# Two 512-token chunks of an MLP mixer joined into one of 1024 tokens, on one core

## Chip, cores and metric

The kernel runs on one core of a Trainium2 chip. The metric is the device time of one execution in microseconds (us); runs of a kernel are summed up by their median. An execution can also be profiled: the profile's span runs from the first to the last instruction of the program, and the execution's own time lies a little above it.

## What is computed

Memory attention for 8 batches of 576 tokens, then a token-mixing and a channel-mixing layer. The change lies in the channel mixing (the last line) and in the order of the work at the start of the program.

```python
# _attn_ref, per batch and head: 32 memory slots from phi, k, v; softmax attention of q over the slots
x = attn_out.transpose(0, 2, 1, 3).reshape(8, 576, 512)
xt = x.transpose(0, 2, 1)
h = np.maximum(xt @ w_tok1, 0.0) @ w_tok2          # token mixing, 576 -> 256 -> 576
u = x + h.transpose(0, 2, 1)
h2 = np.maximum(u @ w_ch1, 0.0) @ w_ch2            # channel mixing, 512 -> 1536 -> 512
return u + h2
```

## The kernel before

**Chunks.** The 8 x 576 = 4608 tokens are cut into 9 chunks of 512 (`CW`), numbered 0 to 8; `HW` is 256. For each chunk the channel mixing runs layer 1 (512 to 1536 channels, in 12 hidden blocks of 128, taken as 6 pairs `p`) and layer 2 (back to 512). Each product is written in float32 as three matmuls on halves: high x high, high x low, low x high. ScalarE (ACT) makes a high half by a copy, VectorE (DVE) the low half by a subtraction. TensorE (PE) is the engine that all of this feeds; its sums stand in PSUM banks of 512 float32 columns.

**Three forms.** Chunks 0 to 2 (`Chunk`) multiply plainly, with matmuls of 512 columns (lines 159 and 182). Chunks 3 to 6 (`Quarters`) do layer 1 by seven quarter products instead of eight: a block matrix of two by two, with sums and differences of the blocks (Winograd's form: products named 11, T1, 21, T2, 22, T3, T4), which take 256 columns, half of the chunk's tokens, each (line 320); layer 2 stays plain. Chunks 7 and 8 (`Sevens`, driven by `seven`) do both layers by seven products of 256 columns: layer 1 at line 420 into one PSUM tile `one`, layer 2 at line 373 into the tiles `m` and `mT`. For each pair, layer 1 of the pair is interleaved on PE with layer 2 of the pair before it (`mix`). Layer 2 of the last pair of chunk 8 is plain (line 402). A quarter product is 6 matmuls: two halves of 128 of its inner or its output side, times the three combinations.

**Sums of weights.** Seven products need sums of the weights too. Those of `w_ch1` are made once (`Sums`), stored in DRAM and loaded per pair as units (`load_unit`, 3 ahead). Those of `w_ch2` (`Tops`, four blocks a pair, each in high and low) are made by DVE and ACT from half-step 156 on and stay in rooms of SBUF that other tiles have left.

**Order.** From the first product on, a half-step counter `h` orders the work by hand: `at(h, fn)` puts a step at a half-step, `MOVES` shifts single steps, and each step is recorded on its engine's queue in that order. There are 24 half-steps a chunk, 4 a pair; chunk 7 begins at half-step 168. The split of the chunk's input into blocks and halves (`t1` to `t4`, `high`, `low`) stands in the 15 half-steps ahead of the chunk. Before the first product, in the front, a planner inside the program (`plan`) orders some 390 steps (the attention of batches 0 and 1, the weights' unpacking): it holds a cost for each step and picks, at each turn, the free step of the highest rank. Ranks came from seeded draws (`SEEDS`). Where it sees PE idle, it puts filler matmuls of the identity (line 1242).

Of the kernel before, what the change touches and what calls it, by code (L numbers as in the profile page):

```python
# [10 lines left out]
F32 = mybir.dt.float32  # L11
# [9 lines left out]
P = 128  # L21
# [7 lines left out]
def kernel(  # L29
# [188 lines left out]
    class Quarters(Chunk):  # L218
# [3 lines left out]
        def __init__(s, c):  # L222
            s.c, s.n, s.hid, s.x = c, f"_{c}", {}, {}
            s.u = s.o = wide(F32, "u" + s.n)
            s.end = NF - (2 if c == CHUNKS - 1 else 0)
# [99 lines left out]
    class Sevens(Quarters):  # L325

        banks = {}  # L330
        rooms2 = {}

        def left(s, name, p):
            if name in s.tops[p]:
                return s.tops[p][name]
            i, j = {"11": (0, 0), "21": (0, 1), "T4": (1, 1)}[name]
            return [x[p][:, j, HW * i : HW * i + HW] for x in (c2h, c2l)]

        def open_banks(s):
            tags = [(pat, "at", 2)] * 2 + [(pacc, f"acc{a}", 1) for a in range(NKK)] + [(pch, "ch", 2)]  # L340
            for name, (pool, tag, n) in zip(("11", "22", "T1", "T3", "T2", "21", "T4"), tags):
                s.banks[name] = pool.tile([P, 2, HW], F32, tag=tag, name="m" + name, bufs=n)

        def open_rooms(s):
            r = s.rooms2
            for name, tag in (("st2", "hh"), ("st3", "hl"), ("11", "hh"), ("22", "hl"), ("21", "al"), ("V", "al")):
                r[name] = sb.tile([P, 2, HW], F32R, tag=tag, name="r" + name, bufs=2)
            for name, tags in (("T13", ("ah", "ah")), ("T24", ("Rh", "Rl"))):
                r[name] = [
                    sb.tile([P, 2, HW], F32R, tag=tag, name=f"r{name}{x}", bufs=2 if tag == "ah" else 1)  # L350
                    for x, tag in enumerate(tags)
                ]
            for name, x in (("T1", 0), ("T3", 1), ("T2", 2), ("T4", 3)):
                r[name] = [t[:, x % 2] for t in r[("T13", "T24")[x // 2]]]
            Sevens.T = {
                name: sb.tile([P, HW], F32, tag=tag, name="s" + name, bufs=1)
                for name, tag in (("T1", "Ah"), ("T3", "Al"), ("T2", "vb"))
            }

        def right(s, name):  # L360
            r = s.rooms2[name]
            return (r[:, 0], r[:, 1]) if name[0] != "T" else r

        def seconds(s, p):

            for name in ("11", "22", "T1", "T3", "T2", "21", "T4"):
                lh, ll = s.left(name, p)
                h, l = s.right(name)
                for a in range(2):
                    for x, (l_, r) in enumerate(((lh, h), (lh, l), (ll, h))):  # L370
                        first, last = not (a or x or p), a == 1 and x == 2
                        yield name if last else None, lambda name=name, a=a, l_=l_, r=r, first=first: (
                            nc.tensor.matmul(  # L373
                                s.banks[name][:, a], l_[:, a * P : a * P + P], r,
                                start=first, stop=False, skip_group_check=True,
                            )
                        )

        def drain(s, name):
            V, m = f32(s.rooms2["V"]), s.banks  # L380

            def add(to, x):
                o = s.quarter(int(to[0]) - 1, int(to[1]) - 1) if to != "V" else V
                return lambda: nc.vector.tensor_tensor(out=o, in0=x, in1=o, op=ALU.add)

            return {
                "11": [lambda: nc.scalar.copy(out=V, in_=m["11"]), add("11", m["11"])],
                "22": [add("12", m["22"])],
                "T1": [add("12", m["T1"]), add("22", m["T1"])],
                "T3": [],  # L390
                "T2": [add("V", m["T2"]), add("12", V), add("V", m["T3"]), add("22", V), add("21", V)],
                "21": [add("11", m["21"])],
                "T4": [add("21", m["T4"])],
            }[name]

        def direct(s, i, t, fs, ps, start=False):

            for a in range(2):
                for n, f in enumerate(fs):
                    h, l = s.hid[f]  # L400
                    for x, (l_, r) in enumerate(((c2h, h), (c2h, l), (c2l, h))):
                        nc.tensor.matmul(
                            ps[:, a],
                            l_[f // 2][:, f % 2, (2 * i + a) * P : (2 * i + a + 1) * P],
                            r[:, t * HW : (t + 1) * HW],
                            start=start and not (a or n or x), stop=False, skip_group_check=True,
                        )

        def first(s, ps, weights, name, start):
            mm = [  # L410
                (l[:, a], r[:, a])
                for a in range(2)
                for l, r in (
                    (weights[:, 0], s.x[name][0]),
                    (weights[:, 0], s.x[name][1]),
                    (weights[:, 1], s.x[name][0]),
                )
            ]
            for n, (l, r) in enumerate(mm):
                nc.tensor.matmul(ps, l, r, start=start and n == 0, stop=False, skip_group_check=True)  # L420

    class Tops:
# [5 lines left out]
        def words(s):  # L428
            s.w = sb.tile([P, 2, DM], F32, tag="big", name=f"cw{s.p}", bufs=1)
            for j in range(2):  # L430
                yield lambda j=j: nc.vector.tensor_tensor(
                    out=s.w[:, j], in0=f32(c2h[s.p][:, j]), in1=f32(c2l[s.p][:, j]), op=ALU.add
                )

        def rooms(s):
            def quad(pool, tag):
                return pool.tile([P, 4, HW], F32R, tag=tag, name=f"top{tag}", bufs=1)

            if s.p in (0, 5):
                tag = ("kv", "rest")[s.p // 5]  # L440
                t = sb.tile([P, 2, 4, HW], F32R, tag=tag, name=f"top{tag}", bufs=1)
                s.pieces = [(t[:, 0, o], t[:, 1, o]) for o in range(4)]
                s.merged = [(t[:, 0, o : o + 2], t[:, 1, o : o + 2]) for o in (0, 2)]
            elif s.p < 3:
                h, l = (quad(wp, f"w{s.p}{x}") for x in "hl")
                s.pieces = [(h[:, o], l[:, o]) for o in range(4)]
                s.merged = [(h[:, o : o + 2], l[:, o : o + 2]) for o in (0, 2)]
            elif s.p == 4:
                h = quad(sb, "qT")
                l = [  # L450
                    sb.tile([P, HW], F32R, tag=tag, name=f"top{tag}{x}", bufs=2)
                    for tag in ("vh", "vl") for x in range(2)
                ]
                s.merged = None
                s.pieces = [(h[:, o], l[o]) for o in range(4)]
            else:
                s.merged, s.pieces = None, []
                for x, (tag, n) in enumerate((("phi", 2), ("phi", 2), ("S", 1), ("aT", 1))):
                    t = sb.tile([P, 2, HW], F32R, tag=tag, name=f"top{tag}{x}", bufs=n)
                    s.pieces.append((t[:, 0], t[:, 1]))  # L460
            Sevens.tops[s.p] = dict(zip(("T2", "T3", "22", "T1"), s.pieces))

        def steps(s):

            yield from s.words()
            s.rooms()
            a11, a21, a12, a22 = w = [s.w[:, j, HW * i : HW * i + HW] for j in range(2) for i in range(2)]
# [7 lines left out]
            parts = [(h, l, x) for (h, l), x in zip(s.pieces, w)]  # L475
            if s.merged:
                parts = [
                    (h, l, s.w[:, j].rearrange("p (i n) -> p i n", i=2)) for j, (h, l) in enumerate(s.merged)
                ]
            for h, l, x in parts:  # L480
                yield lambda h=h, x=x: nc.scalar.copy(out=h, in_=x)
            for h, l, x in parts:
                yield lambda h=h, l=l, x=x: nc.vector.tensor_tensor(out=l, in0=x, in1=f32(h), op=ALU.subtract)

    Sevens.tops = {}
    chunks = {}

    def mixer(c):
        if c not in chunks:
            chunks[c] = (Chunk if c < WIN else Quarters if c < CHUNKS - 2 else Sevens)(c)  # L490
        return chunks[c]
# [1976 lines left out]
```

## Time and profile before

| what | value |
| --- | --- |
| median of 3 runs | 745.89 us (745.12 to 746.94) |
| the profiled execution: its own time, its span | 746.36 us, 744.5 us |
| PE, DVE, ACT, POOL busy | 736.8, 518.3, 371.0, 84.0 us |
| PE instructions | 5387 |
| granted TensorE clock | 0.9 of full speed or more in each of 40 slices |
| DMA | 147.40 MB, mean 198 GB/s |

PE, DVE, ACT and POOL are TensorE, VectorE, ScalarE and GpSimd; PEld is TensorE's loading of weights, which overlaps its matmuls; SP issues DMAs. A matmul's duration in a row is longer than its turn on the engine, since matmuls are pipelined: its price is read from the distance between the starts of equal ones. The same holds, with a smaller overlap, for DVE and ACT.

### The profile page before, as it was taken

What the parts mean: (1) busy time and instruction counts of PE and PEld (TensorE: products, weight loads), DVE (VectorE), ACT (ScalarE), POOL (GpSimd) and SP (SyncE); (2) the same over time, 40 slices, a digit from 0 to 9 for tenths busy, and PEclk for the clock granted to TensorE, in tenths of its full rate; (3) what the DMA queues carried; (4) which work ended last, traced back from release to release, by engine and by line L of the source; (5) the groups of instructions that cost most, each with busy time, mean ns of one, the idle gap of its engine ahead of it and who ended that gap; (6) DMA issues with size and microseconds to landing.
All of it is one profiled execution on the core that took longest, in us unless ns stands there. A gap on an engine that the chain in (4) does not pass through costs nothing.

```text
span 744.5 us, 14081 instructions
## 1 busy us (share of the span) xinstructions
PE 736.8 (99%) x5387; PEld 655.3 (88%) x5387; DVE 518.3 (70%) x1032; ACT 371.0 (50%) x845; POOL 84.0 (11%) x79
## 2 busy tenths in 40 slices
PE   8999999999999999999999999999999999999997
PEld 8787788787878888998998989888989999999997
DVE  4989864788567757774776568664856478889646
ACT  5889774242414334553644436353635354656452
POOL 1114434002112122000000000000001000000000
PEclk9999999999999999999999999999999999999999
DMA  8965540575826355786777858683756467656741
GB/s 351 396 234 190 198 126 11 145 249 168 280 54 229 108 182 180 243 229 216 183 251 226 270 150 274 202 268 120 217 204 188 117 182 252 207 160 206 245 150 57
DMA packets 90835, 147.40 MB, mean 198 GB/s; under 512 B 41488, under 2 KB 61072, under 8 KB 86544
## 3 DMA queue, kind: packets, MB, share of 16 engines
q1 hardware_dynamic: 74496, 99.81, 41.1%
q10 hardware_dynamic: 16272, 46.68, 20.0%
q8 instruction: 43, 0.70, 0.4%
q14 instruction: 24, 0.20, 0.1%
HBM read 121.57 MB, written 24.90 MB: 197 GB/s over the span
## 4 chain that ended last, share of the span: by engine, by line
PE 95%; DMA 2%; DVE 2%; SPq 0%; issue 0%; ACT 0%; DVEq 0%
PE acc L182 31%; PE cp L159 13%; PE qa L320 9%; PE one L420 8%; PE u L908 8%; PE qb L320 7%; PE mT L373 4%; PE Ap L868 3%; PE m L373 3%; PE Rp L887 1%; PE sp L725 1%; DMA kv<-in_kv_dram 1%; PE sp L626 1%; PE u L1566 1%; PE kvp L626 1%; DMA rows<-S 1%
## 5 line engine op out<-in xcount | busy, mean ns | idle before, releaser
L182 PE MATMUL acc<-qhh,c 128*128 128x512 f32 x256 | 99.2, 396 | 0.0
L182 PE MATMUL acc<-hh,c 128*128 128x512 f32 x288 | 96.6, 394 | 0.0
L320 PEld LDWEIGHTS qa<-xT,unit 128*128 128x128 f32 x432 | 61.1, 188 | 6.5 <-ACT whole L2140 0.3
L320 PEld LDWEIGHTS qb<-x,unit 128*128 128x128 f32 x432 | 61.1, 188 | 6.3
L182 PEld LDWEIGHTS acc<-hh,c 128*128 128x128 f32 x288 | 54.1, 188 | 14.1 <-issue 2.9
L320 PE MATMUL qa<-xT,unit 128*128 128x256 f32 x432 | 62.9, 281 | 0.0
L320 PE MATMUL qb<-x,unit 128*128 128x256 f32 x432 | 62.8, 281 | 0.0
L182 PEld LDWEIGHTS acc<-qhh,c 128*128 128x128 f32 x256 | 48.2, 188 | 9.3 <-issue 3.3
L182 PE MATMUL acc<-hl,c 128*128 128x512 f32 x144 | 56.2, 390 | 0.0
L182 PE MATMUL acc<-qal,c 128*128 128x512 f32 x192 | 54.5, 394 | 0.0
L2143 DVE TENSOR_TENSOR whole<-whole 128x256 f32<-128x256 f32 x48 | 20.6, 430 | 44.5 <-ACT whole L2140 44.5
L159 PE MATMUL cp<-uh,c1h 128*128 128x512 f32 x144 | 51.5, 398 | 0.0
L182 PE MATMUL acc<-qhl,c 128*128 128x512 f32 x128 | 50.7, 396 | 0.0
L2140 ACT COPY whole<-qa 128x256 f32<-128x256 f32 x72 | 26.7, 371 | 48.1 <-PE qa L320 46.1
L159 PE MATMUL cp<-ul,c1h 128*128 128x512 f32 x144 | 50.3, 390 | 0.0
L159 PE MATMUL cp<-uh,c1l 128*128 128x512 f32 x144 | 50.3, 390 | 0.0
L127 DVE SCALAR_TENSOR_TENSOR hl<-cp,hh 128x512 fp32r<-128x512 f32 x36 | 24.8, 688 | 30.3 <-ACT hh L124 30.2
L420 PE MATMUL one<-x,unit 128*128 128x256 f32 x288 | 40.5, 283 | 0.0
L420 PEld LDWEIGHTS one<-x,unit 128*128 128x128 f32 x288 | 37.3, 192 | 0.4 <-ACT whole L2292 0.2
L2140 ACT COPY whole<-qb 128x256 f32<-128x256 f32 x48 | 17.8, 370 | 38.4 <-PE qb L320 38.4
L182 PEld LDWEIGHTS acc<-qal,c 128*128 128x128 f32 x192 | 32.2, 189 | 2.9
L925 ACT COPY rest<-u 128x288 f32<-128x288 f32 (+8 forms) x48 | 15.3, 318 | 37.6 <-PE u L908 36.8
(343 smaller groups left out, 1812.4 us busy)
## 6 DMA issues: line engine op xcount, KB each, us to landing
unit<-sums ACTq DMA_DIRECT2D x75, 512.0 KB, 4.1
unit<-sums SPq DMA_DIRECT2D x33, 512.0 KB, 4.4
kv<-in_kv_dram SPq DMA_DIRECT2D x12, 1280.0 KB, 8.2
rawc<-in_w_ch_dram SPq DMA_DIRECT2D x12, 1024.0 KB, 7.1
q<-in_q_dram SPq DMA_DIRECT2D x16, 576.0 KB, 6.5
unit<-sums ACTq DMA_DIRECT2D x25, 256.0 KB, 3.7
sums<-sums SPq DMA_DIRECT2D x12, 512.0 KB, 5.7
phi<-in_phi_dram SPq DMA_DIRECT2D x16, 320.0 KB, 4.8
```

The costliest lines, as they stand in the source:

```text
L127: nc.vector.scalar_tensor_tensor(out=l, in0=ps, scalar=0.0, in1=f32(h), op0=ALU.max, op1=ALU.subtract)
L159: nc.tensor.matmul(ps, l[:, a, w], r[:, a], start=n == 0, stop=n == len(mm) - 1)
L182: nc.tensor.matmul(ps, l_[f // 2][:, f % 2, a * P : (a + 1) * P], r[:, w], start=f == start and x == 0, stop=f == end - 1 and x == 2,)
L320: nc.tensor.matmul(ps[:, :HW], l, r, start=first and n == 0, stop=n == len(mm) - 1, skip_group_check=not first,)
L373: nc.tensor.matmul(s.banks[name][:, a], l_[:, a * P : a * P + P], r, start=first, stop=False, skip_group_check=True,)
L420: nc.tensor.matmul(ps, l, r, start=start and n == 0, stop=False, skip_group_check=True)
L626: nc.tensor.matmul(s.kvp[32 * i : 32 * i + 32, : 2 * D], s.pt[:, i, j, :], s.kv[:, :, j, i, :], start=j == 0, stop=j == NC - 1,)
L868: nc.tensor.matmul(ps[:, :TT], a, w, start=x == 0, stop=x == len(mm) - 1)
L908: nc.tensor.matmul(ps[:, :HALF], a, r, start=x == 0, stop=x == len(mm) - 1)
L925: nc.scalar.copy(out=rest[0][:, kk, o : o + HALF - n], in_=ps[:, n:HALF])
L2140: nc.scalar.copy(out=to, in_=ps[:, :HW])
L2143: nc.vector.tensor_tensor(out=to, in0=x, in1=y, op=ALU.add)
```

## The change

Chunks 7 and 8 are taken as one pair of chunks (`Pair`, 1024 tokens): the two column blocks of the seven products are the two chunks, so a quarter product has 512 columns. First layer 1 of all six pairs `p` runs (line 393 of the changed file), and its results `hid` stay in SBUF, 24 tiles of 512 columns; then layer 2 runs (`second`, line 2233), 42 steps `k` of two groups of three matmuls. Right sides of layer 2 are split into high and low by `prepare`, 6 steps ahead (`LEAD`). Chunk 8's input and output live in the tile `rest`. `Tops` now stores its blocks in DRAM; pair 0's are made in the half-steps ahead of layer 1, the others during layer 1, and `load_tops` brings all of them back once layer 2 has begun. In the last product (T4) the second output half runs as two pieces of 256 columns.

The planner takes a fixed rank and engine for each step (`RANKS`) in place of drawn ones, with other costs for DMA and overlap; the count of fillers follows a new formula, and some entries of `MOVES` change.

```diff
-    class Sevens(Quarters):
...
+    class Pair(Quarters):
...
+        def quarter(s, k, t):
+            return (s.u, rest[0])[t][:, 2 * k : 2 * k + 2]
...
+        def product(s, ps, weights, name, first, end):
             mm = [
-                (l[:, a], r[:, a])
+                (l[:, a], r[a])
                 for a in range(2)
...
+                    ps, l, r, start=first and n == 0, stop=n == len(mm) - 1,
...
+                    for x, t in enumerate((h, w)):
+                        nc.sync.dma_start(out=tops[s.p][:, x, o], in_=f32(t))
...
-    def plan(seeds):
...
+    OVERLAP = {"ACT": 0.09, "DVE": 0.07}
+
+    def plan(ranks):
...
-                landed = max(landed, z.begin + 2.2) + 1.08 * z.move
+                landed = max(landed, z.begin + 2.2) + 0.91 * z.move + 1.6 * (z is first_loads[2])
...
+    RANKS = (
+        778, 776, 772, 756, 780, 770, 774, 754, 748, 704, 702, 554, 728, 446, 366, 102,
...
+    PAIR = [
+        (-15, "t1"), (-15, "high", "11"), (-14.5, "high", "T1"), (-13, "low", "11"), (-10.5, "low", "T1"),
+        (-6.5, "t3"), (-6, "high", "21"), (-5.5, "t2"), (-5, "high", "T3"), (-4, "high", "T2"), (-4, "low", "T3"),
+        (-3.5, "low", "21"), (-3, "t4"), (-2.5, "high", "22"), (-2.5, "low", "T2"), (-2, "high", "T4"),
+        (-1.5, "low", "22"), (-1, "low", "T4"),
+    ]
...
-        shares = (12, 12, 12, 12) if begin else (11, 11, 11, 9)
...
+    STEPS = (("11", "U"), ("T1", "B"), ("21", "A"), ("T2", "U"), ("22", "B"), ("T3", "U"), ("T4", "D"))
+    TOPS, banks, LEAD = {}, {}, 6
+
+    def second(k, a, w=slice(0, CW)):
+        (name, room), p = STEPS[k // (NF // 2)], k % (NF // 2)
+        (lh, ll), r = left_rows(name, p), ring[k]
+        h, l = r[:, 0, w], r[:, 1, w]
+        for x, (l_, r_) in enumerate(((lh, h), (lh, l), (ll, h))):
...
+    def last_part(p):
+        a = start_a.pop()
+        first(p, 6, a, "T4", False)
+        relu(hid["21", p], a)
...
+        first(p, 1, b1, "21", True)
+        if p:
+            add(hid["22", p - 1], start_a[0], hid["22", p - 1])
...
+        if p:
+            last_part(p - 1)
...
+        a = pch.tile([P, CW], F32, tag="ch", name=f"m11{p}", bufs=2)
+        first(p, 0, a, "11", True)
+        nc.scalar.copy(out=hid["11", p], in_=a)
+        add(hid["11", p], b1, hid["11", p])
...
+        b2 = pat.tile([P, CW], F32, tag="at", name=f"mT1{p}", bufs=2)
+        first(p, 3, b2, "T1", True)
...
+        first(p, 2, a, "T2", False)
+        nc.scalar.copy(out=hid["12", p], in_=a)
...
+        first(p, 5, b2, "22", False)
...
+        first(p, 4, a, "T3", False)
...
+    for k in range(6 * n):
+        for a in range(2):
+            second(k, a)
+        if k == 1:
+            last_part(p)
+            load_tops()
...
+        prepare(k + LEAD)
+        for fn in side.pop(k, ()):
+            fn()
```

Where it moves instructions shows at three places. First PE, in the last stage: pair 1 of chunk 8 before, layer 1 of the joined chunks (`m`, `mT`) and the begin of layer 2 (`mU`) in the change; `c` and `top...` are weights, `r`, `rT`, `x` and `xT` right sides.

```order
L373 MATMUL m_6982<-r_6875,topw2h 128x256 x2
L373 MATMUL m_6982<-r_6875,topw2l 128x256
L373 MATMUL mT_6983<-rT_6878,topw2h 128x256
L373 MATMUL mT_6983<-rT_6879,topw2h 128x256
L373 MATMUL mT_6983<-rT_6878,topw2l 128x256
L420 MATMUL one<-x_7_6856,unit_7226 128x256 x6
L420 MATMUL one<-xT_7_6809,unit_7200 128x256 x6
L373 MATMUL mT_6983<-rT_6879,topw2h 128x256
```

```order
L393 MATMUL m_7089<-x_6398,unit_7010 128x512 x6
L393 MATMUL mT_7101<-xT_6410,unit_7034 128x512 x6
L393 MATMUL m_7089<-xw1h,unit_7034 128x512
L393 MATMUL m_7089<-xw1l,unit_7034 128x512
L2233 MATMUL mU_7384<-r_7343,c_578 128x512 x3
L2233 MATMUL mU_7385<-r_7343,c_578 128x512 x3
L2233 MATMUL mU_7384<-r_7353,c_701 128x512 x3
```

Each matmul has 512 columns instead of 256, and the two layers no longer take turns.

Second DVE, at pair 5 of chunk 6, just ahead of the stage that is changed: before, and in the change. L2143 and L2120 (`whole`) and L127 (`qhl`, `qal`) are chunk 6's own steps, L265/L274 and L365/L380 split the next input, the rows with `cw`, `cvh` and `cvl` make `Tops`.

```order
L2143 TENSOR_TENSOR whole<-whole 128x256
L274 TENSOR_TENSOR x_7_6696<-u_6107,x_7_6696 128x512
L127 SCALAR_TENSOR_TENSOR qhl_6_6752<-whole,qhh_6_6751 128x256
L265 TENSOR_TENSOR t_6393<-t_6393,u_6107 128x512
L483 TENSOR_TENSOR topw1l<-cw_6683,topw1h 128x512
L265 TENSOR_TENSOR t_6393<-u_6107,t_6393 128x512
L483 TENSOR_TENSOR topw1l<-cw_6683,topw1h 128x512
L2143 TENSOR_TENSOR whole<-whole 128x256
```

```order
L380 TENSOR_TENSOR x_6398<-u_6110,xphi_6700 128x512
L127 SCALAR_TENSOR_TENSOR qhl_6_6759<-whole,qhh_6_6758 128x256
L365 TENSOR_TENSOR t_6396<-u_6110,t_6396 128x1024
L434 TENSOR_TENSOR cvh_6704<-cvh_6704,cAh_6708 128x256
L434 TENSOR_TENSOR cvh_6705<-cvh_6705,cAl_6709 128x256
L380 TENSOR_TENSOR xw1l<-t_6396,xw1h 128x1024
L2120 TENSOR_TENSOR whole<-whole 128x256
L434 TENSOR_TENSOR cvl_6706<-cvl_6706,cvb_6710 128x256
L2120 TENSOR_TENSOR whole<-qb_6_6783,whole 128x256
L127 SCALAR_TENSOR_TENSOR qal_6_6761<-whole,qal_6_6760 128x256
L380 TENSOR_TENSOR xw2l<-rest,xw2h 128x1024
L127 SCALAR_TENSOR_TENSOR qhl_6_6759<-whole,qhh_6_6758 128x256
```

Steps of the split are twice as wide (1024 for 512), and more of them stand between chunk 6's own steps.

Third PE in the front, from batch 0's scores (`sp_0_0`) to batch 1's (`sp_0_1`): before, and in the change. `kp_1` are batch 1's keys, `Tp_1` turns them, `vp_0` are batch 0's values; products with `ident` alone are fillers.

```order
L1459 MATMUL sp_0_0_220<-kb_0_218,q_0_108 128x64 x8
L1406 MATMUL kp_1_238<-k_1_110 32x64 x20
L1242 MATMUL Tp_1_272<-ident 128x128 x5
L1435 MATMUL Tp_1_272<-ident,T_1_269 128x128
L1242 MATMUL sp_0_1_285<-ident 128x128 x2
L1459 MATMUL sp_0_1_285<-kb_1_279,q_1_112 128x64 x8
L1406 MATMUL vp_0_302<-kv_0_106,pt_0_159 32x64 x20
```

```order
L1411 MATMUL sp_0_0_221<-kb_0_218,q_0_114 128x64 x8
L1358 MATMUL kp_1_239<-k_1_116 32x64 x20
L1194 MATMUL vp_0_273<-ident 128x128 x4
L1358 MATMUL vp_0_273<-kv_0_112,pt_0_167 32x64 x20
L1387 MATMUL Tp_1_302<-ident,T_1_270 128x128
L1194 MATMUL sp_0_1_313<-ident 128x128 x5
L1411 MATMUL sp_0_1_313<-kb_1_309,q_1_118 128x64 x8
```

Batch 0's values now stand ahead of batch 1's keys and scores, and the fillers between are nine where they were seven.

## Rows read from the trace of the kernel before

**Rows 1.** The page's part 1: span; busy time, share, instructions.

```profile
span 744.5 us, 14081 instructions
PE 736.8 (99%) x5387; PEld 655.3 (88%) x5387; DVE 518.3 (70%) x1032; ACT 371.0 (50%) x845; POOL 84.0 (11%) x79
```

**Rows 2.** Busy by window: length, PE, PEld, DVE, ACT, POOL (instructions), clock, DMA.

```profile
720.00:740.00 20.00, 20.00 (x169) 20.00 (x168) 14.15 (x32) 7.89 (x20) 0.00 (x0) 1.00 0.09 28
```

**Rows 3.** Timeline, last 9 us: start, duration, engine, line, operation, out<-in.

```profile
736.31 1.60 PE L402 MATMUL free<-hid,c 128*128 128x256 f32 x12
...
737.75 1.60 PE L402 MATMUL m<-hid,c 128*128 128x256 f32 x12
...
739.19 1.60 PE L402 MATMUL mT<-hid,c 128*128 128x256 f32 x12
...
740.83 0.76 DVE L2379 TENSOR_TENSOR u<-mT,u 128x256 f32<-128x256 f32 x2 [0.74 <-PE mT L402]
```

**Rows 4.** All of line 420: duration min/median/max in ns, first and last start.

```profile
L420 PE MATMUL one<-x,unit x288: 277/283/388, 613.2 to 729.5; 128*128 128x256 f32 x144
L420 PE MATMUL one<-xT,unit x216: 277/283/284, 618.8 to 734.0; 128*128 128x256 f32 x108
```

**Rows 5.** The chain that ended last: start, time, line, instructions of 512 columns.

```profile
70.04 2.72 PE cp L159 x12
```

**Rows 6.** Timeline of PE in chunk 6's last pair.

```profile
606.15 0.86 PE L182 MATMUL acc<-qal,c 128*128 128x512 f32 x3
606.85 0.87 PE L320 MATMUL qb<-x,unit 128*128 128x256 f32 x6
```

**Rows 7.** Timeline of DVE: widths 1024, then 512 and 256.

```profile
43.47 1.23 DVE L989 SCALAR_TENSOR_TENSOR rawc<-rawc 128x1024 f32<-128x1024 f32 x1 [0.64 <-ACT rawc L978]
44.62 1.23 DVE L972 SCALAR_TENSOR_TENSOR rawc<-rawc 128x1024 int32<-128x1024 int32 x1
...
612.75 0.68 DVE L274 TENSOR_TENSOR xT<-t,xT 128x512 fp32r<-128x512 f32 x1
613.36 0.42 DVE L474 TENSOR_TENSOR cw<-cw 128x256 f32<-128x256 f32 x1
613.69 0.68 DVE L274 TENSOR_TENSOR xT<-t,xT 128x512 fp32r<-128x512 f32 x1
```

**Rows 8.** Groups by line: busy us, mean ns of one, idle before.

```profile
L200 DVE TENSOR_TENSOR u<-acc,u 128x512 f32<-128x512 f32 x16 | 10.9, 688 | 8.0 <-PE acc L182 8.0
L2306 ACT COPY rst<-one 128x512 f32<-128x512 f32 x12 | 7.0, 587 | 14.9 <-issue 10.3 <-PE one L420 3.1 <-DVE rT L2273 0.8
```

**Rows 9.** Busy by window, chunk 6's last pair.

```profile
604.00:612.00 8.00, 8.00 (x53) 7.28 (x52) 5.90 (x12) 4.80 (x12) 0.00 (x0) 1.00 0.53 143
```

**Rows 10.** The page's DMA issues: count, KB, median us to landing.

```profile
unit<-sums ACTq DMA_DIRECT2D x75, 512.0 KB, 4.1
```

**Rows 11.** Timelines of PE, DVE and POOL in the front.

```profile
18.14 2.37 PE L1459 MATMUL sp<-kb,q 128*128 128x64 f32 x20
20.44 0.77 PE L1406 MATMUL vp<-kv,pt 128*32 128x64 f32 x40
...
29.65 0.63 PE L1514 MATMUL at<-ident,k 128*128 128x128 f32 x4 [1.26 <-DVE k L1505]
...
42.22 1.17 PE L159 MATMUL cp<-uh,c1h 128*128 128x512 f32 x4
...
21.99 0.88 DVE L1483 TENSOR_REDUCE mx<-sp 128x16 f32<-128x512 f32 x2
...
25.41 1.59 DVE L984 TENSOR_SCALAR raww<-raww 128x576 int32<-128x576 int32 x1
...
28.68 0.82 DVE L1505 TENSOR_TENSOR k<-k,sm 128x640 f32<-128x640 f32 x1
...
31.83 0.69 DVE L984 TENSOR_SCALAR rawc<-rawc 128x1024 int32<-128x1024 int32 x1
...
25.19 1.50 POOL L1000 TENSOR_TENSOR w2l<-raww,w2h 128x576 fp32r<-128x576 f32 x1 [5.94 <-ACT w2h L996]
```

More of the change, by code (lines that the diff above doesn't have):

```diff
@@ L323, in product @@
                 )
-    class Sevens(Quarters):
[L330 to L409, printed above, removed]
@@ L1170, in when @@
             for y in z.after:
-                t = max(t, y.end if y.eng == z.eng else y.ready)
+                t = max(t, y.end if y.eng == z.eng and not y.lands else y.ready)
             more = {}
@@ L1946 @@
                 break
-            gap = z.begin - max(idle, 2.0)
-            if gap > 0.3 and z.take:
-                late = any(y.eng == "SP" and y.ready > z.begin - 0.5 for y in z.after)
-                z.fill = int(0.85 * gap / 0.24) + 3 * late
+            begin = max(idle, 2.0)
+            if z.begin - begin > 0.3 and z.take:
+                cold = max(min(z.begin, 5.1) - idle - 1.6, 0.0)
+                pace = 0.222 if z.begin < 12.0 else 0.24
+                z.fill = int(cold / 0.43 + 0.9 * (z.begin - max(begin, 5.1)) / pace)
             idle = z.end
@@ L2090, with top_step @@
         at(2 * NF * WIN - 4 + n, load_unit, n, k=1)
-    for p, h in enumerate((156, 161, 166, 173, 180, 187)):
-        top = Tops(p).steps()
-        for x in range(14 if p in (3, 4) else 10):
-            at(h + x / 2, lambda top=top: next(top)(), k=1, key=("top", p, x))
+    top0 = []
+    def top_step():
+        if not top0:
+            top0.append(Tops(0).steps())
+        next(top0[0])()
+    for x in range(16):
+        at(2 * NF * (CHUNKS - 2) - 6 + x // 3, top_step, k=1, key=("top", x))
     def run(h, *ks):
@@ new lines, with first, mix @@
+    todo = [(x, f, a) for x, f in before for a in range(NKK)]
+    start_a, unit0 = [], 4 * (CHUNKS - 2 - WIN) * (NF // 2)
+    def first(p, k, ps, name, start):
+        n = unit0 + 4 * p
+        if k in (1, 0, 2, 4):
+            load_unit(n + {1: 0, 0: 1, 2: 2, 4: 3}[k] + AHEAD)
+        pair.product(ps, units[n + k // 2][:, k % 2], name, start, True)
+    def mix(n=2):
+        for x, f, a in todo[:n]:
+            x.ch2(f, [a])
+            if f == x.end - 1:
+                x.add(a)
+        del todo[:n]
@@ L2286, in seven @@
-        if left:
-            left.pop()()
-        product(1, "21", b, True)
-        if begin:
-            nc.scalar.copy(out=st1[:, 1], in_=b)
-        else:
-            nc.scalar.copy(out=st1, in_=X)
-        mix(shares[0])
-        if not begin:
-            high("22", c22)
-            T_high("T1")
-            T_high("T3")
-            low("22", c22)
-            T_low("T1")
-            T_low("T3")
-            sub(T["T4"], st1[:, 0], T["T2"], True)
-        drain(3)
-        events_at(0, 0.5)
@@ L2346, in seven @@
-        drain(3)
-        events_at(3, 3.5)
-        def rest():
-            ch.first(a, units[n + 3][:, 0], "T4", False)
-            load_unit(n + 3 + AHEAD + 1, nc.sync)
-        if end:
-            rest()
-            mix(99)
-            relu_high(oh[:, t0], a)
-            relu_low(oh[:, t0], ol[:, t0], a)
-            assert not stream, stream
-        else:
-            left.append(rest)
-        return ch, p
-    for c in range(CHUNKS - 2, CHUNKS):
-        for p in range(NF // 2):
-            before = seven(c, p)
@@ new lines @@
+        first(p, 3, b2, "T1", True)
+        nc.scalar.copy(out=hid["22", p], in_=b2)
+        if p < NF // 2 - 1:
+            extra += Tops(p + 1).steps()
+        else:
+            extra += [lambda k=k: prepare(k) for k in range(4)]
+        more(3 if p < NF // 2 - 1 else 1)
+        mix()
+        events_at(1.5, 2)
+        first(p, 2, a, "T2", False)
+        nc.scalar.copy(out=hid["12", p], in_=a)
+        more(3 if p < NF // 2 - 1 else 1)
+        mix()
+        events_at(2.5)
+        first(p, 5, b2, "22", False)
@@ new lines @@
+        more(2 if p < NF // 2 - 1 else 1)
+        add(hid["12", p], b2, hid["12", p])
+        events_at(3)
+        first(p, 4, a, "T3", False)
+        more(1)
+        events_at(3.5)
+        start_a.append(a)
+    p = NF // 2 - 1
+    add(hid["22", p], start_a[0], hid["22", p])
+    relu(hid["22", p], hid["22", p])
+    nc.vector.scalar_tensor_tensor(
+        out=hid["12", p], in0=hid["12", p], scalar=0.0, in1=hid["11", p], op0=ALU.max, op1=ALU.subtract
+    )
+    for k in range(4, LEAD):
+        prepare(k)
@@ new lines @@
+    end = [pch.tile([P, CW], F32, tag="ch", name=f"mD{a}", bufs=2) for a in range(2)]
+    end.append(pat.tile([P, CW], F32, tag="at", name="mD2", bufs=2))
+    for x, w in enumerate((slice(0, CW), slice(0, HW), slice(HW, CW))):
+        a = min(x, 1)
+        banks["D"] = [end[x]] * 2
+        for k in range(6 * n, 7 * n):
+            second(k, a, w)
+            if not a:
+                for fn in side.pop(k, ()):
+                    fn()
+        read("21", "D", a, w)()
+        put("21", slice(a, a + 1), w, nc.scalar if w.start else nc.sync)()
```

448 lines of the change are left out of this document (226 added, 222 removed), and 29 rows, old and new, of tables (RANKS, SEEDS).

## Prediction, made before the changed kernel ran

> **What bounds the kernel now.** The page first: PE is busy in 736.8 of 744.5 us, DVE in 518.3 [rows 1]. A modelled busy time does not say whether PE runs at its pace, so I read windows next: in the last stage 169 matmuls fit in 20 us with no idle time and the clock at 1.00 [rows 2]. Equal matmuls in a row then give the pace: groups of 12 of 256 columns start 1.44 us apart, 120.0 ns each [rows 3]. So from its first product at 42.22 us [rows 11] until the last matmul, PE is the bound, and a change pays what it takes out of PE's own time, out of the front before 42.22, or out of the tail behind the last matmul.
>
> The stage that changes starts at 613.2 us [rows 4]. Its matmuls of 256 columns: 7 products x 6 matmuls x 12 pairs = 504 in layer 1 (the 288 + 216 of rows 4), 42 x 11 = 462 in layer 2, and 4 quarters x 12 = 48 plain ones at the end, together 1014. At 120.0 ns that is 121.7 us.
>
> **The matmuls.** The change keeps the columns nearly equal and doubles the width. Layer 1: 42 x 6 = 252 of 512 columns. Layer 2: 252 of 512, of which 18 run as 36 of 256. So 486 wide and 36 narrow. What a wide one costs stands in the trace where nothing else is between: 12 in 2.72 us, 226.7 ns, each with weights of its own [rows 5]. Among narrow ones it is dearer: three in 0.70 us, 233 ns [rows 6]. The new stage is all wide, so it is nearest to rows 5; I take 228. Then 486 x 228 + 36 x 120 = 115.1 us, a gain of **6.6 us**; the two rows bound it at 7.2 (226.7) and 4.1 (233). Per column a narrow matmul pays 0.469 ns and a wide one 0.445: what is saved is a part that each instruction pays, whatever its width, some 13 ns (2 x 120.0 - 226.7).
>
> The Trainium skill (TensorE: Matmul & The Clock Gate, Back-to-back issue gap) gives a warm gap of N/2.4 + 2.5 ns, by which that part is far smaller; an estimate by it makes the old stage 110.7 us, the new one 108.8, and the gain 1.9. Both rows lie above it (109.2 and 215.8 by the Trainium skill), so here the rows decide.
>
> **What must hide behind it.** Layer 1, a pair: seven groups of 6 wide matmuls, 7 x 1.37 = 9.6 us of PE. DVE has, by order, 8 steps of 256, 4 of 512 and one of 1024 columns. From start to start these take 0.33, 0.61 and 1.15 us [rows 7]: 6.2 us. One PSUM bank is handed over three times a pair (11 to T2, T2 to T3, T3 to T4), each time with another group of 1.37 us between; the reading takes 0.59 for a copy on ACT or 0.69 for a sum on DVE [rows 8], so 0.7 us of cover are left. I count nothing for it.
>
> Between the layers, six right sides are ready ahead, and the first loads of `Tops` wait for rooms that the last pair's products leave. The first is needed eleven groups, 15 us, after product 11 of pair 5 frees its room; a load of the same 512 KB lands in 4.1 us [rows 10]. In layer 2 a step is 1.37 us of PE; DVE's densest stretch, steps 14 to 25, is 12 x 2 x 0.61 plus four sums of 0.61, 17.1 us against 16.4. The 0.7 us come out of a lead of six steps (8.2 us). Nothing counted.
>
> Ahead of layer 1 it is tighter. In chunk 6's last pair DVE has, by the order shown, five steps of 1024, four of 512 and 16 of 256: 5.75 + 2.4 + 5.3 = 13.5 us, while PE needs 42 x 0.120 + 24 x 0.23 = 10.6 us. Before, the stretch had 5.90 of 8.00 [rows 9]. DVE so comes out 3 us late. What PE reads first of the late work (a low half for the first mix, one group of 1.37 us into the stage) still comes in time, by my count with some 0.5 us to spare; the last split (T4) is needed only in the second pair. I put **0.6 us** of stalls for all this, between 0 and 3.
>
> **The tail.** Now two DVE sums of 0.76 us together follow the last matmul [rows 3]; after the change one of 256 columns, 0.42 [rows 7]. Gain **0.3 us**; the DMA behind it has the same 128 KB.
>
> **The front.** Behind the wait that ends at 29.65, PE has nothing but its own work up to 42.22, the same work in the changed order plus two fillers, so the front moves with that wait. It is for batch 1's softmax, whose last step DVE starts at 28.68 [rows 11]. Two things move it. Batch 1's scores come later: they end after 18.14 + 2.37 = 20.5 now; with the values (0.70) and two fillers more ahead of them, and their keys' mask step behind other work on DVE, I count 22.6. But DVE takes up the scores only at 21.99 now, so 0.8 us of the delay count, not 2.1. Against that, DVE does a 0.4 us step of the values earlier, and the step of 1.59 us at 25.41 may run in its usual time: a wider one takes 0.69 [rows 11], and the slow one coincides with POOL's step at 25.19. In the change that POOL step waits for ACT's cast, which now stands behind batch 1's exponential, so it should meet a reduction instead. The sum is 0.8 - 0.4 - 1.2 = -0.8; PE itself is ready at about 29.1, so **-0.4** is left. Bounds: -1.3 (all idle time before 29.65, 1.26) and +2.1 (the scores' delay in full). That the weights then keep pace with PE after 42 rests on PE having waited for none of them before.
>
> **Sum.** 744.5 - 6.6 - 0.3 - 0.4 + 0.6 = 737.8 span. The profiled execution took 746.36, 1.86 above its span, so 739.7; it lies 0.5 above the median of the runs, 745.89, so **739.2 us**.
>
> **Rivals.**
> - *DVE's lateness reaches PE.* If the 3 us at chunk 6's end fall on what PE reads next, the stage starts 3 us later instead of 0.6: 741.6. The 13.5 against 10.6 speaks for it; against it, that most of the late steps are splits which PE needs one to several groups later. It decides once the 0.5 us are gone.
> - *The front loses.* If the scores' 2.1 us come through in full, 739.2 + 0.4 + 2.1 = 741.7. DVE's late arrival at the scores speaks against it; for it, that nine fillers, not seven, stand ahead of them.
> - *The bank's handing over stalls layer 1, and the kernel is slower.* Layer 2 no longer fills PE between layer 1's products, so only one group covers each of 18 handings over. Should the reading engine come 1.1 us later than I count, at each, 18 x (1.1 - 0.7) = 7.2 us, in place of the 0.6, eat the gain: 745.8; at 1.3 us it is 10.8 and 749.4, slower. It decides at about 1.1. DVE being in order speaks for it, with up to four narrow steps (1.3 us) ahead of a sum; against it, DVE's 6.2 of 9.6 us.
> - *Columns cost, not instructions; the change brings no gain.* If a wide matmul with float32 halves from freshly written tiles paid 0.469 ns a column, 486 x 240 + 4.3 = 121.0 us, a gain of 0.7: 745.1. Rows 5 speak against it.
> - *The fixed part is small.* A gain of 1.9 in place of 6.6 would give 743.9. It needs a narrow matmul at 109 ns, which rows 3 exclude. The Trainium skill's formula (TensorE: Matmul & The Clock Gate, Back-to-back issue gap) would have it so.
>
> **Chances.** My forecast, within some 2 us either way, 0.70; DVE's lateness 0.11; the front 0.09; the handing over 0.05, of which 0.02 end slower, 0.02 near no change and 0.01 faster; no gain per column 0.02; the small fixed part 0.01; something else 0.02, evenly. What this kernel's measurement can tell from no change is about 0.2%, 1.5 us. So faster 0.93, the same 0.04, slower 0.03. The range for 8 in 10: the low end takes the gain at 7.2 and the front at -1.3 without stalls (744.5 - 7.2 - 0.3 - 1.3 + 1.86 - 0.5 = 737.1, and a little for the overhead): 736.8. The high end takes in the first two rivals and part of a gain at 4.1 us (739.2 + 2.5 = 741.7): 742.2.
>
> **What would show it.** Wide matmuls in the last stage 227 to 229 ns apart in runs of six and more; about 115 us from layer 1's first matmul to the last, chunk 6's remaining 5.5 us aside. PE waiting nowhere in that stage, or else before layer 1's first groups for DVE. The wait for batch 1's softmax ending at 29 to 29.5 and the first product at 41.5 to 42. One sum behind the last matmul. I am wrong if the wide matmuls lie near 233 ns, if gaps stand at T2, T3 or T4 in layer 1, if step 6 of layer 2 waits for a DMA, or if the first product starts after 43.

## The result, and the profile after

The changed kernel takes 737.59 us (median of four runs, 736.41 to 737.79), beside 745.98 us for the kernel before on the same chip (median of four, 745.12 to 746.94): a ratio of 0.9886 with a 95% interval of 0.9868 to 0.9905. Timed again on another chip it took 737.23 beside 745.08, 0.9895 (0.9882 to 0.9908). It is faster by about 8 us; 739.2 was predicted, with 736.8 to 742.2 as the range.

Part 1 of the page after, to be held against [rows 1]:

```profile
span 735.8 us, 12841 instructions
PE 728.6 (99%) x4889; PEld 627.8 (85%) x4889; DVE 506.6 (69%) x944; ACT 356.4 (48%) x759; POOL 83.0 (11%) x77
```

PE has 498 fewer matmuls, 492 of them in the last stage, and is still busy in 99% of the span. The page can't say where 8.7 us of span went, since a modelled busy time hides the pace. The last stage can, in one window from its first matmul to the end of its last (columns as in [rows 2]):

```profile
611.79:732.44 120.65, 120.65 (x547) 99.60 (x545) 87.76 (x154) 51.09 (x83) 0.00 (x0) 1.00 0.59 207
```

Before, the same stage ran from 613.16 (613.2 in [rows 4]) to 739.19 + 1.60 = 740.79 [rows 3], 127.63 us. So it gives 6.98 us at the same full clock. In steady running the pace is seen in 20 us of layer 2:

```profile
700.00:720.00 20.00, 20.00 (x90) 16.57 (x89) 17.24 (x29) 9.54 (x16) 0.00 (x0) 1.00 0.13 53
```

There were 169 matmuls of 256 columns in 20 us [rows 2]; now there are 90 of 512, both counts with those that an edge cuts. By the starts of single matmuls, layer 2's wide ones lie 226.7 ns apart on average and its narrow ones 119.8, so 512 columns cost 226.7 in place of 240.0 ns. PEld, busy all the time before, is now at 83%.

The end, in the timeline of the changed kernel, beside [rows 3]:

```profile
728.32 4.12 PE L2233 MATMUL mD<-rT,c 128*128 128x256 f32 x33
...
732.48 0.42 DVE L2205 TENSOR_TENSOR u<-mD,u 128x256 f32<-128x256 f32 x1 [1.73 <-PE mD L2233]
732.93 0.37 ACTq L2359 DMA_DIRECT2D out_dram<-u  x1
```

One sum of 0.42 us follows the last matmul instead of two in 0.76. From the last matmul's end to the span's end it is 3.35 us (735.79 - 732.44), before 3.72 (744.51 - 740.79): 0.37 gained.

The whole ledger of the two profiled executions, before minus after: first product 42.22 - 41.83 = 0.39; from there to the start of the last stage 0.98 (613.16 - 611.79 = 1.37 in all by then); last stage 6.98; tail 0.37; together 8.72, the difference of the spans. The stage and the tail were foretold; the 0.98 was not. It lies almost wholly at one place. The waits of the kernel before, 485 to 500 us (waiting engine and line, what it waited for, us, times, longest):

```profile
ACT nat L120 <- DMA raw<-rows: 2.2, 1, 2.2
...
PEld Ap L868 <- ACT nat L120: 0.9, 1, 0.9
```

A batch's rows come back from memory late, ACT's cast waits, and PE's step Ap stands behind it. After, PE waits for nothing there. Either the moved events did this, or that wait belongs to one execution: a question for the experiments.

One wait is new in the last stage. Of the changed kernel's waits from 611 to 676 us this is the only one that stops PE's weight loads:

```profile
PEld mT L393 <- ACT hid L2318: 1.2, 5, 0.2
```

Its place in the timeline, in the third pair of layer 1 (L2311 copies product 11 to SBUF, the sum on L2205 and the relu on L2208 belong to it; L2318 copies T1, whose bank product 22 needs; mT<-xT is T1, mT<-xw2h and mT<-xw2l are 22):

```profile
629.47 1.52 PE L393 MATMUL mT<-xT,unit 128*128 128x512 f32 x6
629.67 0.59 ACT L2311 COPY hid<-m 128x512 f32<-128x512 f32 x1 [0.76 <-PE m L393]
630.29 0.69 DVE L2205 TENSOR_TENSOR hid<-m,hid 128x512 f32<-128x512 f32 x1 [2.27 <-ACT hid L2311]
...
631.02 0.63 ACT L2208 ACTIVATE hid<-hid 128x512 f32<-128x512 f32 x1 [0.76 <-DVE hid L2205]
...
631.56 0.57 ACT L2318 COPY hid<-mT 128x512 f32<-128x512 f32 x1
...
631.97 0.39 PE L393 MATMUL m<-xw1h,unit 128*128 128x512 f32 x1
632.18 0.19 PEld L393 LDWEIGHTS mT<-xw2h,unit 128*128 128x128 f32 x1 [0.24 <-ACT hid L2318]
632.19 0.48 PE L393 MATMUL mT<-xw2h,unit 128*128 128x512 f32 x1
...
632.51 0.40 PE L393 MATMUL mT<-xw2l,unit 128*128 128x512 f32 x1
```

T1's last matmul has ended by 630.99, but ACT reads it only at 631.56: the relu ahead of it in ACT's order waits for DVE's sum. The weight load of 22's first matmul, which would start with the matmul ahead at 631.97, waits for the copy's end at 632.13. That first matmul starts on time, at 632.19, but the next one follows after 0.32 us instead of 0.227. The 1.2 us are the weight loads' waiting; the path loses five times 0.09. Pair 0 has no such wait: chunk 6's last products (`mix`) stand between its groups.

### The profile page after: what moved, and what is told of

Its sections match the earlier page's. It is cut to its first block, busy times and chain, and to the rows that moved or that the text cites. A ratio compares the mean times of both kernels' runs of the same rounds, so it can differ in the third digit from the quotient of the medians.

```text
span 735.8 us, 12841 instructions
## 1 busy us (share of the span) xinstructions
PE 728.6 (99%) x4889; PEld 627.8 (85%) x4889; DVE 506.6 (69%) x944; ACT 356.4 (48%) x759; POOL 83.0 (11%) x77
## 4 chain that ended last, share of the span: by engine, by line
PE 97%; DMA 1%; ACT 1%; DVE 1%; SPq 0%; issue 0%
PE acc L182 32%; PE cp L159 14%; PE qa L320 9%; PE u L865 8%; PE qb L320 7%; PE m L393 6%; PE mU L2233 3%; PE Ap L825 3%; PE mT L393 2%; PE mB L2233 2%; PE Rp L844 1%; PE sp L682 1%; PE mD L2233 1%; PE mA L2233 1%; DMA raww<-in_w_tok_dram 1%; PE sp L583 1%
## 5 line engine op out<-in xcount | busy, mean ns | idle before, releaser
L2120 DVE TENSOR_TENSOR whole<-whole 128x256 f32<-128x256 f32 x48 | 20.0, 417 | 43.4 <-ACT whole L2117 43.4
L127 DVE SCALAR_TENSOR_TENSOR hl<-cp,hh 128x512 fp32r<-128x512 f32 x36 | 24.8, 688 | 27.6 <-ACT hh L124 27.5
L865 PE MATMUL u<-w2h,Rh 128*128 128x288 f32 x112 | 33.0, 295 | 0.0
L865 PE MATMUL u<-w2l,Rh 128*128 128x288 f32 x112 | 33.0, 294 | 0.0
```

The source lines that it names most:

```text
L127: nc.vector.scalar_tensor_tensor(out=l, in0=ps, scalar=0.0, in1=f32(h), op0=ALU.max, op1=ALU.subtract)
L865: nc.tensor.matmul(ps[:, :HALF], a, r, start=x == 0, stop=x == len(mm) - 1)
L2120: nc.vector.tensor_tensor(out=to, in0=x, in1=y, op=ALU.add)
```

## The experiments

My theory before the runs: each matmul pays some 13 ns whatever its width, which makes the stage; the front gives some tenths by its new plan; and the rest is hidden, with little to spare. The rivals: the gain comes from the new order of the layers or from less work on other engines; or the 1 us ahead of the stage is a gain of the moved events.

**The same stage in narrow matmuls.** Every wide product of the pair as two halves:

```
-                nc.tensor.matmul(
-                    ps, l, r, start=first and n == 0, stop=n == len(mm) - 1,
...
+                for t in (slice(0, HW), slice(HW, CW)):
+                    nc.tensor.matmul(
+                        ps[:, t], l, r[:, t], start=first and n == 0 and not t.start, stop=n == len(mm) - 1,
...
```

The matmuls of layer 2 in `second` are halved in the same way.

> The changed kernel, with each of the 486 products of 512 columns in the last stage written as two of 256 with the same weights; order, sums and transfers as changed. If each instruction pays a fixed part of 13.3 ns (2 x 120.0 - 226.7), 486 more instructions cost 6.5 us: 744.1 us, and the last stage takes 127.1 us instead of 120.65. If columns cost and instructions don't, it stays at 737.6. If the gain came from the new order of the layers or from fewer steps on other engines, it stays near 737.6 too. If narrow matmuls can go at 109 ns, the stage gains against the change.

Measured: 744.59 us, 0.9992 of before (0.9984 to 1.0001): the whole gain is gone. The stage takes 127.40 us (611.73 to 739.13), 6.75 more than the change's. 20 us of its layer 2:

```profile
715.00:735.00 20.00, 20.00 (x169) 20.00 (x168) 10.19 (x18) 4.98 (x9) 0.00 (x0) 1.00 0.13 53
```

169 matmuls again, as in [rows 2], though order, sums and transfers are the new ones. Two things lie beside the matmuls: this execution lost 0.79 us once, near 636 us, where PE waited for the load of a unit, and the 5 x 0.09 for T1's copy are not in it. Without them it is 6.75 - 0.79 + 0.45 = 6.4 us for 486 instructions, 13.2 ns each. The price per instruction stands; the rivals of order and of columns fall.

**The planner alone.** The kernel before with only the planner, its ranks, costs and fillers, from the change.

> The kernel before with the new planner of the front alone; the last two chunks and the table of moved events stay as before. By the prediction's step on the front, the first product starts 0.4 us earlier than before (41.83 after the whole change, 42.22 before) and the last stage takes what it took before, 127.6 us from its first matmul to its last one's end; about 745.5 us, which timing alone cannot tell from no change. Rival: the front's gain hangs on the rest of the change; then the first product stays near 42.2. The change also began its last stage 1.1 us earlier than the front explains, because PE's wait near 494 us, ahead of the step Ap, was gone. If the event table removed that wait, this kernel still has it (0.4 to 0.6 us in one place); if it is a transfer that lands sooner or later from run to run, it may be here or not, though the program there is the same.

Measured: 744.65 us, 0.9988 (0.9979 to 0.9997), so 0.9 us less than before, with 0.2 to 1.6 as its bounds. The first product starts at 42.00, between the two profiles of the kernel before (42.22, and 41.87 in the next run), so the profile shows no gain of its own; the last stage takes 127.62. The wait near 494 is absent, although the event table is that of before. So the table did not remove it.

**Before once more.** No edit.

> The kernel before once more, unchanged, to see how much of its profile belongs to one execution. In its first profile PE lost about 1 us near 494 us, where the step Ap waited for the rows of one batch to come back from memory, and it waited 0.7 us for the first keys and values before the products kp. None of the four profiles of other kernels with the same program near 494 us has the first wait, and the second went from 0 to 1.7 us among them. If both belong to the execution, the wait near 494 is absent or of another length here, and the first product moves by some tenths from 42.22. If the first belongs to the program of before, it stands here again with about 0.6 us in its first gap, and the change's table of moved events took it away.

Measured: 745.0 us, span 743.15; the stage takes 127.62 us, and nothing waits near 494. The first product starts at 41.87. PE's waits in its front are these:

```profile
PE pp L1242 <- POOL mask L91: 1.6, 1, 1.6
PE at L1514 <- DVE k L1505: 1.2, 1, 1.2
```

The wait for the first keys, 0.7 us in the first profile, is gone, and the wait for batch 1's softmax stays. So the 0.98 us of the ledger belong to the execution that I had as before, and not to the change: of twelve profiles that I have, eleven don't show that wait.

**DVE later by two steps of 1024 at chunk 6's end.**

```
-                nc.vector.tensor_tensor(out=l, in0=x, in1=f32(h), op=ALU.subtract)
+                for _ in range(3 if name == "22" else 1):
+                    nc.vector.tensor_tensor(out=l, in0=x, in1=f32(h), op=ALU.subtract)
```

> The changed kernel, with the subtraction for the low half of quarter 22 in chunk 6's last pair done three times over instead of once: two more steps of 1024 columns on DVE (2.3 us) at the place where the prediction counted DVE 3 us late and put 0.6 us of stalls. After the change nothing stalled there; the low half that the mix reads next ended 0.58 us before PE read it. If DVE has just that to spare, PE stalls 1.7 us at the first mix of the last stage, and the time is 739.3 us. If the spare is a smaller one further on (the split of T4 in the second group of the mix, or the stores of the left sides), more than 1.7. If DVE has more to spare than the trace suggests, no stall and 737.6 us.

Measured: 740.03 us, 0.9926 (0.9912 to 0.9939); the stage takes 122.80, so 2.15 more. The timeline of this kernel shows where:

```profile
611.43 3.73 DVE L381 TENSOR_TENSOR xw2l<-rest,xw2h 128x1024 fp32r<-128x1024 f32 x3
...
615.08 0.42 DVE L127 SCALAR_TENSOR_TENSOR qhl<-whole,qhh 128x256 fp32r<-128x256 f32 x1
...
615.55 0.50 PE L182 MATMUL acc<-qhl,c 128*128 128x512 f32 x1 [1.81 <-DVE qhl L127]
```

The three subtractions start 1.25 us apart, since each waits for the end of the one ahead, so the edit added 2.5 us; all but 0.36 of it reach PE, in one place: the low half for the first mix. The change's own timeline has these 0.36 us, between the end of that half (612.80) and the weight load that needs it:

```profile
612.38 0.42 DVE L127 SCALAR_TENSOR_TENSOR qhl<-whole,qhh 128x256 fp32r<-128x256 f32 x1
...
613.16 0.19 PEld L182 LDWEIGHTS acc<-qhl,c 128*128 128x128 f32 x1
```

The place and the mechanism are those of the prediction, its 0.5 us to spare are 0.36; the 0.58 expected here counted up to the matmul. The prediction's rival of DVE's lateness needed only 0.4 us more to begin to come true.

**The bank handed over later.** T2's product copied twice, and three times:

```
         nc.scalar.copy(out=hid["12", p], in_=a)
+        nc.scalar.copy(out=hid["12", p], in_=a)
```

> The changed kernel; in each of layer 1's six pairs ACT copies T2's product out of its bank twice, so that the bank is handed over to T3 0.59 us later. The prediction gave this handing over 0.7 us of cover beyond the copy; in the trace of the change the copy ends 0.69 us before T3's first matmul. So no stall at T3, and the stage takes 120.65 us as before this edit. Rival: the handing over is already at its limit, as the one from T1 to 22 was; then six stalls of up to 0.6 us, 3.5 us in all, 124.2.

> The same with three copies of T2's product, so that the bank is handed over 1.18 us later. With 0.69 us of cover in the trace, and the 0.1 to 0.4 us that the last experiment showed a matmul to need between the end of what it reads and its start, each of six pairs should stall by 0.6 to 0.9 us: 3.6 to 5.4 us in all, the stage 124.2 to 126.1 us. That is the rival of the prediction in which the handing over eats the gain, and it should set in between the two kernels. Other theory: something else in the pair takes the delay up; then no stall.

Measured: the stage takes 121.41 us with two copies, 0.76 more than the change, and 124.49 with three, 3.84 more (738.63 and 740.96 us, one run each). The two kernels' waits of PE's weight loads for the second and the third copy, first with two:

```profile
PEld m L393 <- ACT hid L2328: 1.4, 5, 0.4
```

and with three:

```profile
PEld m L393 <- ACT hid L2329: 4.5, 5, 1.0
```

Neither theory was exact. The cover ended inside the second copy: not none, not 0.7, but about 0.5 us. The timeline with two copies says why:

```profile
633.21 0.59 ACT L2328 COPY hid<-m 128x512 f32<-128x512 f32 x1
...
633.85 0.19 PEld L393 LDWEIGHTS m<-xah,unit 128*128 128x128 f32 x1 [0.25 <-ACT hid L2328]
633.87 0.48 PE L393 MATMUL m<-xah,unit 128*128 128x512 f32 x1
```

The copy ends at 633.80, in time for the matmul at 633.87, but the matmul's weight load waits for it too. Unhindered it would start with the matmul ahead, 0.23 us earlier, and be hidden. So what has to be in time is the weight load. The rival in which the handing over eats the gain exists, from a delay of about 0.5 us beyond the copy on, and with two copies more it costs 0.77 us in each of five pairs. The sixth is pair 0, where chunk 6's products stand between.

**The tail in one piece.**

```
-    for x, w in enumerate((slice(0, CW), slice(0, HW), slice(HW, CW))):
+    for x, w in enumerate((slice(0, CW), slice(0, CW))):
```

> The changed kernel with the last half of T4 as 18 products of 512 columns instead of 36 of 256, so that one sum of 512 columns and one store of 256 KB follow the last matmul. By the matmuls' price the last matmul ends 0.24 us sooner (36 x 120.0 - 18 x 226.7); the sum behind it takes 0.69 instead of 0.42 us. If the store of twice the bytes lands in the same time, the two cancel and the span stays at 735.8, within 0.1; if its bytes count, the tail grows from 3.35 to about 4 us and the span by 0.4.

Measured: the stage takes 120.41 us, 0.24 less, as the price of matmuls has it; the tail is 3.86 us, 0.51 more. The wider sum is 0.27 of it; the last store, of twice the bytes, lands 2.26 us after its issue instead of 1.92, and the program's end follows it 0.1 us sooner. So the split of the last product is worth 0.27 us. The whole ran 736.75 us in one run, less than the change, because its first product started at 40.44: again the front.

**A faster version.** T1's copy ahead of the relu, and no fillers ahead of the last transposition:

```
         add(hid["11", p], b1, hid["11", p])
-        relu(hid["11", p], hid["11", p])
...
         nc.scalar.copy(out=hid["22", p], in_=b2)
+        relu(hid["11", p], hid["11", p])
...
-            if z.begin - begin > 0.3 and z.take:
+            if 0.3 < z.begin - begin and z.begin < 30.0 and z.take:
```

> The changed kernel with two small edits. One: in layer 1 of the last stage ACT copies T1's product ahead of the relu of quarter 11, not behind it. After the change PE waited 1.2 us in five places for this copy, and the matmuls there start 0.09 us late each; if the relu ahead of the copy is the cause, the five waits go and the stage takes 120.2 us instead of 120.65. Rival: the copy then runs into another wait, or the relu comes late for the step on DVE that reads it; then waits show elsewhere in layer 1. Two: no filler matmuls ahead of the last transposition before the first product (0.44 us of PE in the trace of the change). If PE alone sets the front there, the first product starts at 41.4 instead of 41.83, with the clock still granted at full; rival: PE then waits for what that step reads, and the first product stays at 41.8. Together 736.7 us, 0.9 less than the change.

Measured: 736.31 us, 0.9876 of before (0.9862 to 0.9889). PE and its weight loads wait for nothing in the whole stage, which takes 120.07 us:

```profile
610.05:730.12 120.07, 120.07 (x547) 99.99 (x545) 87.70 (x154) 51.00 (x83) 0.00 (x0) 1.00 0.59 208
```

That is 0.58 less than the change, a little more than the 0.45 expected, since in the change the matmuls right behind the late ones lay up to 236 ns apart too; all wide matmuls of layer 1 now lie 226.7 ns apart on average, 228.9 in the change. The first product starts at 39.95, more than 0.44 earlier: in this execution the first keys had come before PE wanted them. The intervals of this version and of the change overlap, so the timing alone does not separate them; the stage's rows do.

**The keys' load first, and the change again.** On top of the faster version:

```
+    order.remove(a.l_k)
+    order.insert(order.index(loads[0]), a.l_k)
     for z in order:
         now[0] = z
```

> The changed kernel with ACT's copy of T1 ahead of the relu and without the fillers ahead of the first product, as in the run named both; in addition SP issues the first load of keys and values (640 KB) ahead of the first load of weights (1 MB) instead of behind it. Nothing else moves. In eight profiles with the new front the wait of the first key products for that load was 0 to 1.7 us, and the first product follows the first scores by a nearly constant time, 29.0 us (28.9 to 29.1), 0.44 less without the fillers. If this load sets the front, the wait is 0 here and the first product starts at 40.0 or a little earlier, against 41.4 for a late load; about 735.5 to 736.3 us. Rival: the weights, now later by what 640 KB take, some 1.7 us, come late for the step that reads them first (PE at 21 to 22 us, behind 7 us of conversion on ACT and DVE); then PE waits there instead, and the front gains nothing or loses.

> The changed kernel once more, unchanged, on the same chip as the last one, for a comparison of the two and for a second look at its front. Its last stage should take 120.65 us from its first matmul to the end of its last, as in the first profile, with the five waits for the copy of T1; its first product lies where the load of the first keys puts it, between 40.4 and 42.0 us. About 737.3 us.

Measured: 739.49 us, 0.9923 (0.9909 to 0.9936), beside 737.23 for the change on the same chip, so it is not faster. Two of the six executions took 736.85 and 737.51 us, like the change's, at a mean granted clock of 1.000; four took 739.49 to 740.14 at 0.995. No profile holds one of the longer ones, so what made them longer, and whether the edit did, is not shown. The profile, of the execution of 737.51, has the last stage at 120.07 again and the first product at 42.13. PE's waits in its front, behind the 1.6 us at its start:

```profile
PE Tp L1387 <- DVE T L1249: 1.5, 1, 1.5
PE sp L1411 <- DVE kb L1395: 0.4, 1, 0.4
PE vp L1358 <- DMA kv<-in_kv_dram: 0.2, 1, 0.2
```

The wait for the keys is gone, and one of the same length stands in its place. DVE's timeline shows its source:

```profile
11.53 1.23 DVE L929 SCALAR_TENSOR_TENSOR raww<-raww 128x1024 int32<-128x1024 int32 x1 [4.70 <-ACT raww L923]
12.67 0.34 DVE L1249 TENSOR_SCALAR T<-kp,col 128x128 f32<-128x128 f32 x1
```

The keys' step T stands behind the weights' join in DVE's order, and the weights are what comes late now. My rival had the weights late for their reader on PE; it was an engine's order that passed the delay on, to a step that doesn't need them. The change's second profile: stage 120.63, first product at 41.19, with a wait of 1.5 us for the values' load and none for the keys'.

## Why the prediction was right

**The matmuls.** The chosen term was 6.6 us with bounds of 7.2 and 4.1; the stage gave 6.98, and 6.98 + 0.58 = 7.56 without the stalls at T1's copy (above the bound: chunk 6's last 24 matmuls of 512 columns, which now stand among wide ones, gave 0.11 us, and the narrow ones had cost 120.2 ns on average instead of 120.0, 0.2 us in all). Taking 228 ns between the rows was too careful: in an all-wide stage they lie at the lower row, 226.7. The Trainium skill (TensorE: Matmul & The Clock Gate, Back-to-back issue gap) puts the warm gap of an isolated matmul at N/2.4 + 2.5 ns; an estimate by it gave a gain of 1.9 us. The same program with wide and with narrow matmuls shows 13.2 ns per instruction, so for this stream of float32 products, each with weights of its own, the measurement decides against the formula.

**What must hide.** The 0.6 us of stalls were put at the wrong place: DVE's lateness at chunk 6's end cost nothing and left 0.36 us. The 0.45 to 0.58 us that were lost stood in a handing over that the prediction did not list. It counted three a pair, all in bank a. The fourth, T1's bank to product 22, has one group of cover like them, but its reader stands in ACT's order behind a relu that waits for a sum on DVE that waits for the copy of product 11. That chain has two groups of time: it begins with product 11's end, at 629.67, and 0.59 + 0.69 + 0.63 + 0.57 and what lies between end at 632.13, 2.5 us later. The weight load behind it would have started at 631.97. The sign "PE waiting nowhere in that stage" so failed in five places. That the stalls came out near the 0.6 us foretold was luck, since their cause was another.

**The tail.** 0.3 was foretold, 0.37 measured. From the last matmul's end to the last sum's end it is 0.46 us, before 0.79, which is 0.33 of it. The last store has 128 KB in both and lands 1.92 us after its issue, before 1.90, as the prediction had it.

**The front.** The first product came at 41.83, foretold 41.5 to 42, from 42.22. The number agrees by luck: two errors cancel. The step that failed is "the front moves with that wait", with "PE itself is ready at about 29.1", worked out from one execution of the loads. The change's own profile has these rows, to be held against [rows 11]:

```profile
28.83 0.62 PE L1466 MATMUL at<-ident,k 128*128 128x128 f32 x4
...
40.92 0.60 PE L1194 MATMUL pp<-ident 128*128 128x128 f32 x4
41.36 0.71 PE L1245 MATMUL pp<-ident,phi 128*128 128x128 f32 x5
```

Batch 1's transposition starts at 28.83, 0.82 us earlier than the 29.65 of before (29.25 was foretold), and PE no longer waits for batch 1's softmax there. DVE starts the softmax's last step 0.76 us earlier, at 27.92, where 0.8 was foretold. But the four fillers at 40.92, which the prediction named as two and gave no time, take 0.44 us of it back: from the transposition to the first product it is 13.00 us, before 12.57. And when PE comes to the transposition hangs on the loads. PE now waits for the first keys and values: 2.0 us in all in the first profile, between 0.2 and 2.3 over the other eight with the new plan and the loads in this order, and the first product lies between 40.44 and 42.02 with it (39.95 without the fillers). With waits of 0.6 us it starts at 40.44, with 2.0 to 2.3 at 41.80 to 42.02. The old front, in two profiles, starts at 41.87 and 42.22. Executions in which the first 1 MB of weights landed alike compare best: 42.22 against 41.75 to 42.02 where it took 7.9 to 8.1 us, 41.87 against 41.05 at 7.5 and 7.3. So the new plan is worth 0.2 to 0.8 us in these, and 0.9 us (0.2 to 1.6) in the timing of the planner alone.

**The sum.** Stage and tail are 7.35 us by profiles that repeat within 0.03 (127.62 to 127.63, and 120.65 and 120.63); the planner's 0.9 by timing makes 8.2, beside 8.4 and 7.9 in the two comparisons. The forecast of 739.2 was 1.6 us too long: 1.0 of it in the stage (6.6 less 0.6 was foretold, 6.98 measured), 0.1 in the tail, and the rest in the front and in what single executions stand off a median.

## What to carry to other kernels

Where one engine is the bound and has no gaps, count its instructions: the price of one that does not depend on its width is found by two groups of different width in the same trace, and it told this change to 0.4 us. A buffer's cover is to be counted from the end of its last write to the start of its reader's chain, through every instruction that stands ahead of the reader in its engine's order, and up to the weight load and not the matmul. Before a difference of a microsecond is given to an edit, the unchanged kernel is profiled twice.

## What was not expected of the hardware

A matmul whose input comes just in time can start on time and still cost 0.09 us, since its weight load of 0.19 us is no longer hidden: starts 0.32 us apart in place of 0.227, with no idle time in PE's own rows. The first loads do not land alike: among eleven profiles with the first loads in one order, the first 1 MB of weights took from 5.8 to 8.2 us to land, and the wait for the first keys ranged from 0 to 1.7 us. What decides this was not found.
